# Separate slots for loads, half-size and whole staging in the last pass of a two-layer decode step with its gradients

## The chip, the core and the metric

The kernel runs on one core of one Trainium2 chip. The metric is device time in microseconds (us) of one launch; lower is better. The core has four compute engines with queues of their own (PE for matmuls, with its weight loads shown as PEld; DVE; ACT; POOL) and SP, which here only issues the loads. Sixteen DMA engines move data between the memory outside the core (HBM, called "dram" in the profile) and the on-chip memory of 128 partitions. PE writes its results to PSUM banks, from where DVE or ACT must fetch them.

## What is computed

The reference is two layers of a decode step (one token, batch 2), and the gradients of all its inputs. A layer is x + attention(layernorm(x)), then x + MLP(layernorm(x)); both layers use the same weights and the same caches.

```python
def _A_ref(x, k_cache, v_cache, wq, wo):      # x 2x1x1024; caches 2x4x16384x128
    q = (x @ wq) ...                          # 32 query heads on 4 cache heads
    scores = jnp.einsum("bhqd,bhkd->bhqk", q, k) * (Dh ** -0.5)
    p = _softmax(scores, axis=-1)
    o = jnp.einsum("bhqk,bhkd->bhqd", p, v)
    return ... o @ wo

def _B_ref(x, w1, b1, w2, b2):                # w1 1024x3584, w2 3584x1024
    y = _layernorm(x, axis=-1)
    h = _gelu(jnp.einsum("bsd,df->bsf", y, w1) + b1)
    return jnp.einsum("bsf,fd->bsd", h, w2) + b2

x = x + _A_ref(_layernorm(x), ...); x = x + _B_ref(_layernorm(x), ...)   # twice
_out, _vjp = jax.vjp(_f, A_x, A_k_cache, A_v_cache, A_wq, A_wo, B_w1, B_b1, B_w2, B_b2)
return (_out, *_vjp(grad_out))
```

All arrays are bf16. Both caches are 33.6 MB each, and so are their gradients (64 stores of 1 MB in all); the gradients of wq, wo, w1 and w2 are outer products of a few columns (2 layers x batch 2 = 4 columns), 31.5 MB together.

## The kernel before

**A program of pieces.** The kernel is first written down as a list of pieces (`P.emit(fn, uses)`): each piece is a Python function that issues a few instructions, with the chunks that it uses. A *chunk* is up to 1 MB of on-chip memory (128 partitions x 4,096 bf16 columns): a load of a part of a cache or a weight, a staging area for a result on its way out, or a small work area. `Program.keep` then looks where a chunk that is loaded again could stay on chip from its last use to the next: it counts the slots, takes off a reserve (`SPARE`, 5) and what lives at each piece, and keeps the shortest gaps first. `Program.run` walks the pieces, hands out slots and calls the functions. The order of the instructions in each engine's queue is therefore the order of the pieces (`tc.manual_schedule`); waits are put in from what touches what.

**Slots.** There are 15 slots of 1 MB (`slot_tiles`), and two areas of two slots each that are free only until a mark: half of `Et[1]` each until piece 683 and half of `D1t` each until piece 1295. In `run` all chunks stand in one list in the order of their first use, loads and staging alike. As soon as a slot is free, the next chunk of that list takes it, and if it is a load, its DMA is issued on SP's queue there and then. So a staging chunk takes its slot as many pieces ahead of use as a load does, and a load may take a slot that staging has just left; SP then waits until the store has landed, and with it every load behind.

**Passes.** Attention forward for layer 0 and 1 (`attn_fwd`), each followed by the MLP; then backward: the MLP of layer 1, attention of layer 1 (`attn_bwd(1, ...)`), the MLP of layer 0, and the last pass, attention of layer 0 (`attn_bwd(0, ..., outputs=outputs)`). An attention pass goes over the 8 pairs (batch, cache head) in 16 steps each; pass directions alternate (`up`, `down`), so the pair that ends a pass starts the next. In a backward step, `kblock` turns an eighth of a V chunk on DVE (L367) and multiplies it with PE (L380), and `direct` multiplies the K chunk's columns (L405) 16 steps later; `slope` and `exchange` (16 small ACT copies, L414) stand between. The backward blocks of wo and wq are turned with PE (L342) and copied by ACT or DVE (L217, L220).

**Outputs in the last pass.** `outputs(s, ...)` adds pieces to each step s:

- `kv_outputs`: for each pair, 8 chunks of cache gradient. `turn` builds a block (L1000), `unit` multiplies it with the work area `qc` (L1018), `cast_out` takes 512 columns from PSUM to the staging chunk on ACT (L225) or DVE (L228), whichever has less to do, and after 8 units POOL issues a 1 MB store (L1023).
- `dw_units`: weight gradients as outer products. `y_rows` transposes columns to 4 rows (L1034) and copies them to partitions 0 to 3 of a work chunk y (L1035) that `y_zero` has cleared (L1041, POOL); `x_rows` transposes the other factor to X (L1049), copied by ACT or DVE; a unit is one 512-column matmul over all 128 partitions (L1064) and a cast. `pieces_rows` groups 7 or 8 units to one store (L1087). `dbias` sums y's rows for the two biases (L1099, L1100, L1103).
- There are three y: `y1` for dh (gradient of w1), `y2` for the gradients of w2 and wo and for half of wq's, `y3` for the rest of wq's. The pieces of weight gradients wait in a list `bg` and are handed out by a credit of 1.3 or more a step, so that they end some 20 steps after the last cache gradient.

K(7,1) below means chunk 1 (of 4) of the K cache of pair 7; w2(24), wo(20) are the chunks of w2 and wo that start at block 24 and 20 of 128 rows. *Ahead* is a load that is issued and not yet used; a *lead* is the number of pieces between issue and first use.

Of the kernel before, what the change touches and what calls it, by code (L numbers as in the profile page):

```python
# [21 lines left out]
SPARE = 5  # L22
SKEW = 2
LAG_F = 28
LAG_B = 16
# [3 lines left out]
class Chunk:  # L29


    def __init__(self, load=None, key=None):
        self.load = load
        self.key = key
# [17 lines left out]
class Program:  # L52
# [6 lines left out]
    def chunk(self, load=None, key=None):  # L59
        c = Chunk(load, key)  # L60
        self.chunks.append(c)
        return c
# [39 lines left out]
    def run(self, slots):  # L102

        order = sorted((c for c in self.chunks if c.first is not None and c.into is None), key=lambda c: c.first)
        free = list(slots)
        nxt = 0
        for i, (fn, uses) in enumerate(self.ops):
            while nxt < len(order):
                c = order[nxt]
                fits = [s for s in free if s[1] is None or c.last < s[1]]  # L110
                s = min(fits, key=lambda s: 1 << 30 if s[1] is None else s[1], default=None)
                if s is None:
                    break
                free.remove(s)
                c.slot, c.at = s, s[0]
                if c.load is not None:
                    c.load(c.at)
                nxt += 1
            uses = [c.root() for c in uses]
            for c in uses:  # L120
                assert c.slot is not None, f"piece {i}: no slot for its chunk"
            fn()
            for c in uses:
                if c.last == i:
                    free.append(c.slot)
# [4 lines left out]
def kernel(  # L130
# [55 lines left out]
    xwp = ctx.enter_context(tc.tile_pool(name="xwp", bufs=2))  # L186
# [72 lines left out]
    D0t = pers.tile([128, 2 * 1024], BF16, name="ds0")  # L259
    slot_tiles = [pers.tile([128, CH], BF16, name=f"slot{i}") for i in range(NSLOT)]  # L260
# [10 lines left out]
    def columns(name, n):  # L271

        t = vec.tile([128, n * 4 + 124], BF16, name=name)
        V.memset(t[:, n * 4:], 0.0)
        wide[name[0]] = t
        return t[:, 0:n * 4].rearrange("p (j c) -> p j c", c=4)
# [683 lines left out]
    def kv_outputs(pos, g):  # L960
# [3 lines left out]
        qc = P.chunk()  # L964
# [25 lines left out]
        for n, (c, w) in enumerate([(c, w) for c in range(NCH) for w in range(2)]):  # L990
            stg = P.chunk()
# [37 lines left out]
    def y_rows(colT, j0, jn, y, at_):  # L1029

        def f():
            tp = ob().bitcast(BF16)[0:4, 0:jn * 128].rearrange("p (a b) -> p a b", b=128)
            for j in range(jn):
                PE.transpose(tp[:, j, :], colT[:, j0 + j, :], ident[:])  # L1034
            V.tensor_copy(out=y.ap[0:4, at_:at_ + jn * 128], in_=flat(tp))  # L1035
            dve(0.7)

        return f, [y]

    def y_zero(y, n):  # L1040
        return (lambda: GP.memset(y.ap[:, 0:n], 0.0)), [y]  # L1041

    def x_rows(xn, j0, jn, hold):
# [11 lines left out]
    def dw_units(xn, y, y_at, pieces):  # L1055
# [3 lines left out]
        for units, store in pieces:  # L1059
            stg = P.chunk()  # L1060
            for n, (j, c0, cn, at_) in enumerate(units):
                def f(j=j, c0=c0, cn=cn, at_=at_, last=(n == len(units) - 1), stg=stg, store=store):
                    ps = ob()[:, 0:cn]
                    PE.matmul(ps, lhsT=hold[j // 4 * 4][:, j % 4, :], rhs=y.ap[:, y_at + c0:y_at + c0 + cn], start=True,  # L1064
# [4 lines left out]
                todo.append((j, (f, [stg, y])))  # L1069
        res, built = [], set()  # L1070
        for n, (_, u) in enumerate(todo):
            for j, _ in todo[n:n + 4]:
                if j // 4 not in built:
                    built.add(j // 4)
                    res.append(x_rows(xn, j // 4 * 4, 4, hold))
# [3 lines left out]
    def pieces_rows(out_ap, n_in, n_out, c0=0):  # L1079

        rb = max(1, CH // n_out)
        res = []
        for j0 in range(0, n_in // 128, rb):
            units = [(j0 + j, c0 + c, 512, j * n_out + c) for j in range(rb) for c in range(0, n_out, 512)]

            def store(ap, j0=j0):
                GP.dma_start(out_ap[j0 * 128:(j0 + rb) * 128, c0:c0 + n_out].rearrange("(j p) n -> p j n", p=128),  # L1087
                             ap[:, 0:rb * n_out].rearrange("p (j n) -> p j n", j=rb))
# [4 lines left out]
    def dbias(y, y_at, n, out_ap):  # L1093
        c = P.chunk()
        res = []
        for c0 in range(0, n, 512):
            def f(c0=c0):
                ps = ob()[0:1, :]
                PE.matmul(ps, lhsT=ones_bf[:, 0:1], rhs=y.ap[:, y_at + c0:y_at + c0 + 512], start=True, stop=True)  # L1099
                V.tensor_copy(out=c.ap[0:1, c0:c0 + 512], in_=ps)  # L1100
                dve(0.6)
                if c0 + 512 >= n:
                    GP.dma_start(out_ap.rearrange("(o f) -> o f", o=1), c.ap[0:1, 0:n])  # L1103
            res.append((f, [c, y]))
# [119 lines left out]
    early += [y_zero(y1, F)] + [y_rows(dh_all, j0, min(8, FJ - j0), y1, j0 * 128) for j0 in range(0, FJ, 8)]  # L1224
    early += units[40:]
    early += dbias(y2, 0, D, out_9)
    early += dw_units("m", y1, 0, pieces_rows(out_6, D, F))
# [65 lines left out]
```

## Time and profile before

| | us |
|---|---|
| median of 3 runs (1266.1 to 1267.7) | 1266.45 |
| the profiled execution | 1268.7 |
| its span, first to last instruction | 1266.8 |

| busy over the span | us | share |
|---|---|---|
| PE | 931.8 | 74% |
| PEld | 709.6 | 56% |
| DVE | 782.8 | 62% |
| ACT | 590.2 | 47% |
| POOL | 73.2 | 6% |
| loads on SP's queue | 354.46 MB | 72.0% of 16 engines |
| stores on POOL's queue | 98.66 MB | 19.3% of 16 engines |

A row of engines by stage (busy us in a stretch, with the number of instructions in brackets) ends with the TensorE clock that was granted (1.00 is full speed), the mean busy share of the 16 DMA engines, and GB/s. A row of waits reads: the engine, its line, what it waited for; total us, times, longest. In a timeline a row reads: start, duration, engine, line, operation, output<-inputs, and in square brackets the idle time before it with what ended it.

### The profile page before, as it was taken

The page shows a single profiled execution, that of the slowest core. Times are in us where ns is not written, and L with a number is a line of the kernel's source. Part 1 is how long each engine was busy: PE and PEld are TensorE (multiplying, and loading weights), DVE is VectorE, ACT ScalarE, POOL GpSimd, SP SyncE. Part 2 cuts the span into 40 slices and gives each one's busy share as a digit, 9 for nine tenths or more (in the row PEclk, how much of TensorE's full clock was granted, in tenths as well). Part 3 has the DMA queues.
Part 4 walks back from the last instruction along what each step waited for, and adds up shares of the span by engine and source line. Part 5 has one row for each costly group of instructions (what it writes and reads, how often), then busy time and mean ns, then how long its engine had stood idle before and what let it go on. Part 6 is the DMA issues. An engine that isn't in the chain of part 4 may idle for free. (4 is left out here: it accounts for less than half of the span.)

```text
span 1266.8 us, 36604 instructions
## 1 busy us (share of the span) xinstructions
PE 931.8 (74%) x15799; PEld 709.6 (56%) x15809; DVE 782.8 (62%) x1630; ACT 590.2 (47%) x1484; POOL 73.2 (6%) x118
## 2 busy tenths in 40 slices
PE   4556655877865578788758977787787778888885
PEld 4555544777764477678757865454444444444342
DVE  5765662258876224767654466666676567877775
ACT  0411221203323112555543446766676666877764
POOL 0000000000000000000000100200110011111112
PEclk9855555755555557666757988888888788988898
DMA  9999999989999999799998855798999988999966
GB/s 357 413 414 414 413 414 412 378 326 354 411 414 413 413 397 396 278 415 411 415 413 330 326 171 201 279 388 351 365 335 336 374 339 322 375 388 377 346 275 232
DMA packets 97581, 455.44 MB, mean 360 GB/s; under 512 B 7138, under 2 KB 7138, under 8 KB 59148
## 3 DMA queue, kind: packets, MB, share of 16 engines
q1 hardware_dynamic: 80604, 354.46, 72.0%
q0 software_dynamic: 16816, 98.66, 19.3%
q8 instruction: 123, 2.02, 0.6%
q14 instruction: 38, 0.31, 0.1%
HBM read 354.47 MB, written 98.62 MB: 358 GB/s over the span
## 5 line engine op out<-in xcount | busy, mean ns | idle before, releaser
L367 DVE STREAM_TRANSPOSE kT<-slot 128x512 int32<-128x512 int32 x476 | 319.1, 695 | 104.0 <-PE sc L380 92.2
L380 PE MATMUL sc<-qbd,kT 128*128 128x32 bf16 x4096 | 273.7, 226 | 15.9 <-DVE kT L367 11.1
L380 PEld LDWEIGHTS <-kT 128*128 128x128 bf16 x4096 | 221.1, 118 | 59.4 <-issue 24.9
L405 PEld LDWEIGHTS <-slot 128*128 128x128 bf16 x3648 | 148.5, 104 | 132.1 <-issue 48.1
L405 PE MATMUL sb<-xt,slot 128*128 128x8 bf16 x3648 | 167.1, 177 | 64.3 <-DMA slot<-in_A_v_cache_dram 27.8
L225 ACT CAST slot<-sc 128x512 bf16<-128x512 f32 x310 | 177.5, 589 | 77.1 <-PE sc L1018 46.1
L228 DVE CAST slot<-sc 128x512 bf16<-128x512 f32 x213 | 144.5, 681 | 75.5 <-PE sc L1018 40.4
L217 ACT COPY kT<-tp 128x512 int32<-128x512 int32 (+1 forms) x165 | 95.9, 583 | 180.2 <-PE tp L342 168.2
L342 PE MATMUL tp<-ident,slot 128*128 128x128 bf16 x1800 | 171.0, 252 | 8.3 <-DVE kT L220 2.6
L1018 PE MATMUL sc<-slot,blk 128*128 128x512 bf16 x339 | 136.9, 428 | 33.4 <-ACT slot L225 20.4
L342 PEld LDWEIGHTS <-slot 128*128 128x128 bf16 x1800 | 133.6, 114 | 11.6 <-issue 5.6
L414 ACT COPY xt<-ds 32x64 int32<-32x64 int32 x512 | 123.9, 242 | 28.2 <-DVE ds L860 21.6
L581 ACT ACTIVATE e<-sc 128x512 bf16<-128x512 f32 x32 | 19.0, 597 | 228.7 <-DVE sc L578 180.1
L225 ACT CAST slot<-sb 128x512 bf16<-128x512 f32 x156 | 91.9, 589 | 35.8 <-PE sb L1018 14.5
L220 DVE COPY kT<-tp 128x1024 bf16<-128x1024 bf16 (+1 forms) x83 | 53.9, 650 | 82.6 <-PE tp L342 71.8
L1064 PE MATMUL sc<-slot,X 128*128 128x512 bf16 x159 | 66.2, 434 | 24.8 <-ACT slot L225 17.9
L228 DVE CAST slot<-sb 128x512 bf16<-128x512 f32 x105 | 71.6, 682 | 19.5 <-PE sb L1018 8.2
L414 ACT COPY xt<-e 32x128 int32<-32x128 int32 x256 | 75.6, 295 | 3.9
L1018 PE MATMUL sb<-slot,blk 128*128 128x512 bf16 x166 | 71.1, 428 | 5.7 <-DVE slot L228 2.0
L1018 PEld LDWEIGHTS <-blk 128*128 128x128 bf16 x512 | 45.7, 103 | 50.8 <-issue 39.8
L1023 POOL DMA_DIRECT2D out_dram<-slot x64 | 34.2, 535 | 360.5 <-ACT slot L225 226.4
L1064 PEld LDWEIGHTS <-X 128*128 128x128 bf16 x240 | 23.2, 103 | 32.9 <-issue 23.1
(271 smaller groups left out, 894.1 us busy)
## 6 DMA issues: line engine op xcount, KB each, us to landing
slot<-in_A_k_cache_dram SPq DMA_DIRECT2D x110, 1024.0 KB, 16.7
slot<-in_A_v_cache_dram SPq DMA_DIRECT2D x104, 1024.0 KB, 15.6
out_dram<-slot POOLq DMA_DIRECT2D x87, 1024.0 KB, 8.6
slot<-in_A_wq_dram SPq DMA_DIRECT2D x30, 1024.0 KB, 10.4
slot<-in_A_wo_dram SPq DMA_DIRECT2D x27, 1024.0 KB, 13.6
slot<-in_B_w_dram SPq DMA_DIRECT2D x19, 1024.0 KB, 12.1
slot<-in_B_w_dram SPq DMA_DIRECT2D x20, 896.0 KB, 16.0
ds<-in_A_v_cache_dram SPq DMA_DIRECT2D x8, 1024.0 KB, 18.1
```

The lines of the kernel that those rows point to most:

```text
L217: S.copy(out=dst.bitcast(I32), in_=src.bitcast(I32))
L220: V.tensor_copy(out=dst, in_=src)
L225: S.copy(out=dst, in_=src)
L228: V.tensor_copy(out=dst, in_=src)
L342: PE.transpose(tp[:, j, :], t, ident[:])
L367: V.transpose(out=kT[:].bitcast(I32).rearrange("p (w j m) -> p w j m", w=4, j=4), in_=c.ap[:, (i % 4) * 1024:(i % 4 + 1) * 1024].bitcast(I ...
L380: PE.matmul(sc[:, a0:a0 + 4, :, 2 * (i % 4) + q], lhsT=kv[:, 2 * q + w, :, e], rhs=qbd[:, g, 2 * w + e], start=(w == 0 and e == 0), stop=( ...
L405: PE.matmul(acc, lhsT=c.ap[:, n * 128:(n + 1) * 128], rhs=xv[:, i // 4, t // 2, :, 2 * (i % 4) + t % 2], start=(i == 0 and t == 0), stop=( ...
L414: S.copy(out=d[32 * t:32 * t + 32, c0:c0 + cn, j, :], in_=s[32 * j:32 * j + 32, c0:c0 + cn, t, :])
L1018: PE.matmul(ps, lhsT=hold["blk"][:, j, :], rhs=flat(qm(w)[:, (u % 2) * 4:(u % 2) * 4 + 4, :]), start=True, stop=True)
L1023: GP.dma_start((dKv if w == 0 else dVv)[g, :, c * 32:(c + 1) * 32, :], stg.ap.rearrange("p (t d) -> p t d", d=128))
L1064: PE.matmul(ps, lhsT=hold[j // 4 * 4][:, j % 4, :], rhs=y.ap[:, y_at + c0:y_at + c0 + cn], start=True, stop=True)
```

## The change

It touches the planner and the outputs of the last pass.

- Chunks have a kind: "load" (also y and the two rows of outputs), "half" (`qc`, staging of weight and bias gradients) or "full" (staging of cache gradients). A slot has a kind, a first piece and a last piece.
- Of the 15 slots, three are load slots until the first step of the last pass and then six half slots; four are load slots until step 19 of it (`LAG_O - 2`) and then full slots; eight stay load slots. The Et and D1t areas stay as they were.
- In `run` only loads (and y) take slots ahead, in order of first use. A staging chunk takes its slot at the piece that uses it first.
- `keep` counts load slots and load chunks only, and its reserve is 4 instead of 5.
- Weight gradients are stored from half slots: 62 stores of up to 0.5 MB instead of 31 of up to 1 MB. Bias gradients are stored 512 columns at a time: nine stores instead of two.
- y1, y2, y3 become one chunk `Y`, cleared once. Row group q of it (partitions 32q to 32q+3) holds the rows of w2's and wo's gradients (q = 0), dh (q = 1) and dq (q = 2), all columns side by side. So that a matmul over 128 partitions meets only its own group, X has zeros in all other partitions: X is now two lasting tiles `Xt`, cleared by POOL when their group changes, and the copy writes only 4 partitions. The column arrays have 64 zero columns in front so that a transpose can put the 4 columns at partition 32q.

```diff
-SPARE = 5
+SPARE = 4
+N_HALF = 3
+N_FULL = 4
...
     def keep(self, slots, spare):
-        room = [sum(1 for s in slots if s[1] is None or i < s[1]) - spare for i in range(n)]
+        room = [sum(1 for s in slots if s[1] == "load" and (s[3] is None or i < s[3])) - spare for i in range(n)]
...
-            if c.first is None:
+            if c.first is None or c.kind != "load":
                 continue
...
     def run(self, slots):
-        order = sorted((c for c in self.chunks if c.first is not None and c.into is None), key=lambda c: c.first)
-        free = list(slots)
+        order = sorted((c for c in self.chunks if c.first is not None and c.into is None and c.kind == "load"),
+                       key=lambda c: c.first)
+        free = {}
+        for s in slots:
+            free.setdefault(s[1], []).append(s)
         nxt = 0
+
+        def take(c, i):
+            fits = [s for s in free[c.kind] if i >= s[2] and (s[3] is None or c.last < s[3])]
+            s = min(fits, key=lambda s: 1 << 30 if s[3] is None else s[3], default=None)
+            if s is None:
+                return False
+            free[c.kind].remove(s)
+            c.slot, c.at = s, s[0]
+            if c.load is not None:
+                c.load(c.at)
+            return True
+
         for i, (fn, uses) in enumerate(self.ops):
...
+            while nxt < len(order) and take(order[nxt], i):
                 nxt += 1
             uses = [c.root() for c in uses]
             for c in uses:
-                assert c.slot is not None, f"piece {i}: no slot for its chunk"
+                if c.slot is None and c.kind != "load":
+                    take(c, i)
...
-        qc = P.chunk()
+        qc = P.chunk(kind="half")
...
-            stg = P.chunk()
+            stg = P.chunk(kind="full")
...
+    Y = P.chunk()
...
-            tp = ob().bitcast(BF16)[0:4, 0:jn * 128].rearrange("p (a b) -> p a b", b=128)
+            tp = ob().bitcast(BF16)[32 * q:32 * q + 4, 0:jn * 128].rearrange("p (a b) -> p a b", b=128)
...
-            V.tensor_copy(out=y.ap[0:4, at_:at_ + jn * 128], in_=flat(tp))
+            V.tensor_copy(out=Y.ap[32 * q:32 * q + 4, at_:at_ + jn * 128], in_=flat(tp))
...
+    def x_rows(xn, j0, jn, q, hold):
 
         def f():
-            X = xwp.tile([128, 4, 128], BF16, name="X")
+            xn_[0] += 1
+            b = xn_[0] % 2
+            if xq[b] != q:
+                GP.memset(Xt[b][:], 0.0)
+                xq[b] = q
...
-                PE.transpose(tp[:, j, :], wide[xn][:, 4 * (j0 + j):4 * (j0 + j) + 128], ident[:])
-            copy_bf(flat(X[:, 0:jn, :]), flat(tp), 0.36, 0.4)
-            hold[j0] = X
+                c0 = 64 + 4 * (j0 + j) - 32 * q
+                PE.transpose(tp[:, j, :], wide[xn][:, c0:c0 + 128], ident[:])
+            r = slice(32 * q, 32 * q + 4)
+            copy_bf(flat(Xt[b][r, 0:jn, :]), flat(tp[r]), 0.36, 0.4)
+            hold[j0] = Xt[b]
...
-            stg = P.chunk()
+            stg = P.chunk(kind="half")
...
-        rb = max(1, CH // n_out)
         res = []
-        for j0 in range(0, n_in // 128, rb):
-            units = [(j0 + j, c0 + c, 512, j * n_out + c) for j in range(rb) for c in range(0, n_out, 512)]
+        if n_out <= 1024:
+            parts = [(j0, 2, 0, n_out) for j0 in range(0, n_in // 128, 2)]
+        else:
+            parts = [(j0, 1, c, min(2048, n_out - c)) for j0 in range(n_in // 128) for c in range(0, n_out, 2048)]
+        for j0, rb, cb, cn in parts:
+            units = [(j0 + j, c0 + cb + c, 512, j * cn + c) for j in range(rb) for c in range(0, cn, 512)]
...
-    y1, y2, y3 = P.chunk(), P.chunk(), P.chunk()
-    early = [y_zero(y2, CH), y_rows(gM_all, 0, 8, y2, 0), y_rows(gA_all, 0, 8, y2, 1024)]
-    units = dw_units("h", y2, 0, pieces_rows(out_8, F, D))
+    early = [(lambda: GP.memset(Y.ap, 0.0), [Y]), y_rows(gM_all, 0, 8, 0, 0), y_rows(gA_all, 0, 8, 0, 1024)]
+    units = dw_units("h", 0, 0, pieces_rows(out_8, F, D))
...
+        if s == 0:
+            mark("half")()
+        if s == LAG_O - 2:
+            mark("full")()
...
-    slots = [(t[:], None) for t in slot_tiles]
-    slots += [(Et[1][:, i * CH:(i + 1) * CH], marks["e1"]) for i in range(2)]
-    slots += [(D1t[:, i * CH:(i + 1) * CH], marks["d1"]) for i in range(2)]
+    slots = []
+    for i, t in enumerate(slot_tiles):
+        until = marks["half"] if i < N_HALF else marks["full"] if i < N_HALF + N_FULL else None
+        slots.append((t[:], "load", 0, until))
+        if i < N_HALF:
+            slots += [(t[:, j * 2048:(j + 1) * 2048], "half", until, None) for j in range(2)]
+        elif i < N_HALF + N_FULL:
+            slots.append((t[:], "full", until, None))
+    slots += [(Et[1][:, i * CH:(i + 1) * CH], "load", 0, marks["e1"]) for i in range(2)]
+    slots += [(D1t[:, i * CH:(i + 1) * CH], "load", 0, marks["d1"]) for i in range(2)]
     P.keep(slots, SPARE)
```

More of the change, by code (lines that the diff above doesn't have):

```diff
@@ L29, with __init__ @@
 class Chunk:
-    def __init__(self, load=None, key=None):
+    def __init__(self, load=None, key=None, kind="load"):
         self.load = load
+        self.kind = kind
         self.key = key
@@ L57, in __init__, with chunk @@
         self.chunks = []
-    def chunk(self, load=None, key=None):
-        c = Chunk(load, key)
+    def chunk(self, load=None, key=None, kind="load"):
+        c = Chunk(load, key, kind)
         self.chunks.append(c)
@@ L120, in run @@
             for c in uses:
-                assert c.slot is not None, f"piece {i}: no slot for its chunk"
+                if c.slot is None and c.kind != "load":
+                    take(c, i)
+                assert c.slot is not None, f"piece {i}: no {c.kind} slot"
             fn()
@@ L124, in run @@
                 if c.last == i:
-                    free.append(c.slot)
+                    free[c.kind].append(c.slot)
                     c.slot = None
@@ L259 @@
     D0t = pers.tile([128, 2 * 1024], BF16, name="ds0")
+    Xt = [pers.tile([128, 4, 128], BF16, name=f"X{i}") for i in range(2)]
     slot_tiles = [pers.tile([128, CH], BF16, name=f"slot{i}") for i in range(NSLOT)]
@@ L1063, in f @@
                     ps = ob()[:, 0:cn]
-                    PE.matmul(ps, lhsT=hold[j // 4 * 4][:, j % 4, :], rhs=y.ap[:, y_at + c0:y_at + c0 + cn], start=True,
+                    PE.matmul(ps, lhsT=hold[j // 4 * 4][:, j % 4, :], rhs=Y.ap[:, y_at + c0:y_at + c0 + cn], start=True,
                               stop=True)
@@ L1068, in f @@
                         store(stg.ap)
-                todo.append((j, (f, [stg, y])))
+                todo.append((j, (f, [stg, Y])))
         res, built = [], set()
@@ L1074, in dw_units @@
                     built.add(j // 4)
-                    res.append(x_rows(xn, j // 4 * 4, 4, hold))
+                    res.append(x_rows(xn, j // 4 * 4, 4, q, hold))
             res.append(u)
@@ L1232 @@
         k = down[2 * i] % HKV
[L1233 to L1235 removed]
+        late[16 * (2 * i + 1) + LAG_B + 17] = [y_rows(dq_all, k * R, 8, 2, k * 1024)] + dw_units(
+            "n", 2, 0, pieces_rows(out_4, D, 1024, k * 1024))
     bg = list(early)
```

64 lines of the change are left out of this document (25 added, 39 removed).

## The prediction

> **What bounds the kernel now.** I read three views in this order: the page's slices and a table by stage, to see which stage has which limit; the waits of SP's queue and of PE in the last pass; then the clock around one stall. Stages by the lines that run in them: 0 to 500 us the two forward layers with their MLPs, 500 to 690 the backward attention of layer 1, 690 to 745 the backward MLP of layer 0, 745 to 1258 the last pass.
>
> ```profile
> core 0: us, PE busy (x) PEld busy (x) DVE busy (x) ACT busy (x) POOL busy (x), PEclk, DMA share, GB/s
> 275.00:440.00 165.00, 114.76 (x2505) 102.07 (x2504) 113.54 (x236) 47.35 (x144) 0.29 (x1) 0.50 1.00 401
> 500.00:690.00 190.00, 143.12 (x3066) 136.38 (x3065) 117.97 (x270) 95.28 (x314) 0.00 (x0) 0.65 0.97 385
> 690.00:745.00 55.00, 48.54 (x1023) 46.13 (x1020) 26.16 (x71) 20.79 (x36) 4.08 (x2) 0.94 0.71 261
> 745.00:1258.00 513.00, 408.81 (x4552) 228.89 (x4562) 362.49 (x659) 355.68 (x806) 61.29 (x98) 0.86 0.85 326
> ```
>
> The attention passes before 690 us keep the DMA engines full (share 0.97 to 1.00): they end when their bytes have come. 690 to 745 is PE's (48.5 of 55 us). In the last pass nothing is full: DMA 0.85, PE 409 of 513 us, DVE 362, ACT 356. It is made of a chain with stalls, so what counts is which stalls the change removes.
>
> ```profile
> engine line waited for: us in total, times, longest us
> SPq L306 <- DMA out_dram<-slot: 280.7, 29, 18.3
> SPq L311 <- DMA out_dram<-slot: 63.0, 5, 21.9
> ```
> ```profile
> PE sc L1018 <- ACT slot L225: 20.4, 12, 3.8
> PE sc L1064 <- ACT slot L225: 17.9, 8, 3.3
> PE sb L405 <- DMA slot<-in_A_k_cache_dram: 13.5, 5, 5.7
> ```
>
> These are the waits of SP's queue and of PE between 745 and 1258 us. SP issues the loads in order, and 34 times it stands still for 343.7 us in all, because the slot of the next load was last used for staging, whose store has not landed. But of these 344 us PE feels 13.5: the loads run about 55 pieces ahead. PE's two larger rows are ACT's casts queued behind the 16 copies of L414 (4 us each time); the change leaves those.
>
> ```profile
> 950.00:956.50 6.50, 6.27 (x88) 3.90 (x86) 5.81 (x10) 5.08 (x11) 0.53 (x1) 1.00 0.99 354
> 956.50:962.50 6.00, 0.33 (x3) 0.04 (x2) 1.36 (x3) 0.97 (x2) 0.53 (x1) 0.76 1.00 382
> 962.50:964.50 2.00, 2.00 (x26) 1.45 (x27) 0.85 (x2) 0.59 (x1) 0.00 (x0) 0.50 1.01 427
> 964.50:966.50 2.00, 2.00 (x15) 1.10 (x14) 1.26 (x2) 0.99 (x2) 0.53 (x1) 0.52 1.03 404
> 966.50:970.00 3.50, 3.24 (x44) 1.65 (x43) 3.17 (x7) 2.95 (x7) 0.00 (x0) 1.00 0.99 311
> ```
>
> Here PE waits 5.67 us for a K chunk. Afterwards the granted clock is 0.50 for 4 us with PE busy throughout: half of those 4 us, 2 us, is lost once more. The stalls that ended at 867.9 (3.26 us) and 991.4 (2.99 us) are followed by 4 us at 0.50 too.
>
> **1. Loads no longer wait for stores.** I worked through the planner's lists (keep, run) over the pieces in order. For before they give 345 loads, which is the page's count (341 large ones and 4 small), 38 of the last pass's 70 loads behind a store (the trace: 34 waits), and issue a median of 62 pieces ahead of use, 52 at least. The pass has 1,442 pieces in 512 us, 0.355 us each. So a lead of 55 pieces is 19.5 us; a wait of 343.7/34 = 10.1 us leaves 9.4, against 10.0 us from issue to landing (median of K's loads between 780 and 1220 us): just late, now and then, as the five stalls show. By the new rule no load follows a store, the median lead is 89 pieces (31.6 us), the least still 52 (18.5 us), now without the 10 us. Full gain: 13.5 us of stalls, plus 3 x 2 us of half clock, 19.5. The DMA engines limit it: 0.85 x 513 = 436 us of work in this pass, and between 820 and 1200 us their share is already 0.93, so some loads stay late. I take 14; bounds 0 and 19.5.
>
> **2. What is kept.** The reserve falls from 5 to 4 and staging is no longer counted. The lists give 27 kept chunks for 24, 342 loads for 345: gone are K(3,1) in the second forward layer, V(0,1) at the start of the backward one, and w2(24), wo(20), wo(24), V(3,0), which were loaded between 690 and 780 us; added are K(7,1) to K(7,3) early in the last pass. One load costs 1.05 MB/0.414 MB per ns = 2.53 us where DMA is full, so the first two give up to 5.1 us; the next four nothing (DMA share 0.71 and less there); the three added 7.6 us of DMA time, which the 0.85 hides (0.85 becomes 0.865), and which would be on the path if DMA were full. I take 3 gained; bounds 7.6 lost and 5.1 gained.
>
> **3. Kept chunks cost depth.** Chunks loaded ahead fall from 12 to 8 in the middle of the backward pass of layer 1 (pieces 1600 to 1700) and from 5-6 to 4 at its end; from 5 to 4 in the first MLP. I cost it at nothing: a lone 1 MB load lands in 4.8 us (740 to 785 us) and takes 2.53 us of full-rate time, so 3 in flight suffice. If not, it is the third rival.
>
> **4. One Y, lasting X.** Three memsets of Y (3.51 us for 4,096 columns, 3.10 for 3,584, 1.82 for 2,048) become one. The first hides in POOL's 31 us of idle time before 722 us; the third did not:
>
> ```profile
> 1241.05 1.82 POOL L1041 MEMSET slot<- 128x2048 bf16 x1
> 1242.91 0.68 DVE L1035 COPY slot<-sc 4x1024 bf16<-4x1024 bf16 x1 [3.17 <-POOL slot L1041]
> 1243.64 0.59 PE L1064 MATMUL sc<-slot,X 128*128 128x512 bf16 x1 [3.75 <-DVE slot L1035]
> ```
>
> POOL reaches it behind a store, DVE waits, PE stands for 3.75 us with nothing else left to do. I take 3 gained (bounds 0 and 4.8, with the half clock). Added are 8 memsets of X, two at each change of row group. From the three rows, (3.51-1.82)/2048 = 0.83 ns a column, so 0.55 us each, behind at most a store's 0.77 us. The copy into X, with the casts behind it on ACT or DVE and the matmuls that need those banks, waits for it. The pieces of X come up to four units before use; the first two memsets meet idle POOL. I take 2 lost; bounds 0 and 8 x 3.75 = 30. The four copies of dh now write rows of a Y that L1064 is reading, and hold the next L1064 for about 0.7 us each as at 748 us: 1 lost, bounds 0 and 3.
>
> **5. Half stores.** 31 gradient stores become 62 and two bias stores nine: 38 issues more on POOL, 0.77 us each (L1087), 29 us, hidden by POOL's idle time (61 of 513 us busy). Without that cover it would be 29 us. Nothing is queued behind them but other stores and the X memsets. The bytes are the same: DMA time 0 more, if it goes by bytes. Matmuls, casts and copies keep their number and width; the copy of X moves 4 partitions instead of 128 at the same width, so 0.
>
> **6. Staging taken late.** A cache chunk gets one of four whole slots at its first use; by the lists at least 47 pieces (16.7 us) after that slot's last store was issued, a gradient piece 46. Stores land in 8.9 us (median), 15.4 at most. So no wait: 0. If landings grew past 16.7 us the casts on ACT and DVE would wait instead of SP.
>
> **Sum:** -14 -3 -3 +2 +1 = -17 us. The profiled execution took 1268.7 us (span 1266.8 and 1.9 around it), 2.25 above the median of 1266.45, to which I apply the difference: 1249.
>
> **The rivals.**
> *A wait takes the place of the one removed* (chance 0.18). With SP unleashed the engines fill, stores land later than 16.7 us, ACT and DVE wait in L225 and L228; or loads stay late because DMA is full. For it: share 0.93 in the middle, store landings up to 15.4. Against it: 436 us of DMA work in 513. Then term 1 is nothing, and terms 2 and 4 remain: 1266.5 - 3 = 1263 (1260 to 1266).
> *More is gained than PE's row shows* (0.07): DMA idles at 0.42 to 0.64 between 740 and 780 us and around 810; earlier loads there also smooth later stretches. All bounds at their best: 19.5 + 5.1 + 4.8 = 29, or 1237.
> *Slower: too little depth at the turns* (0.17). In pieces 1773 to 1821 the leads fall from 62-91 to 24-48. At 0.343 us a piece (501 pieces in 172 us) 25 pieces are 8.6 us. The loads of wq between 545 and 640 us land in 16.6 us. If that stayed so with four in flight, the first is 8 us late, and four per 16.6 us is 4.15 us a chunk against 2.53: 12 chunks x 1.6 = 19. The turn of the first MLP (15 chunks) adds up to 24, of which PE's own pace hides about half. 8 + 19 + 12 = 39, less the 14 + 3 - 3 of the last pass, less nothing of term 2: 1291, or 1276 if only the later turn suffers. It decides from the point where four in flight no longer fill the engines. Against it: landings follow the number in flight, 19.9 us at about eight, 4.8 alone.
> *Half a store costs the engines a whole one's time* (0.04). Stores of 86.99 MB take 48.7% of 440 us (780 to 1220 us), 2.46 us per MB; the 31.5 MB of weight gradients 77 us. Twice that brings the pass's work to 436 + 77 = 513, all of its length: with the idle starts some 1290. For it: 4 KB stores still take 3.9 us to land. Against it: that is time to landing, not engine time, and 896 KB and 1,024 KB land in the same 8.6 us. The Trainium skill ("DMA: Bandwidth & Descriptors", Bandwidth, Measured) advises batches of 1 MiB or more for three quarters of the peak, and its Anatomy of one DMA gives a fixed 2.0 us per transfer: by that, an estimated 31 x 2 = 62 us if nothing overlapped them. The stores here overlap with loads at a share of 0.93, and no run here shows half ones yet.
>
> **How the numbers follow.** Forecast 0.54: 1249, own range 1240 to 1258. The range to the other cases: 1234 (all bounds at best, a little beyond) to 1278 (the slower rival with one turn); beyond it lie most of two-turn starvation, the half stores and a rest, under 2 in 10. 0.2% is 2.5 us, about what this kernel's measurement can tell from none. Faster than 1263.9: 0.54 + 0.07 + 0.10 of the first rival = 0.71; same: the first rival's other 0.07; slower: 0.17 + 0.04 + 0.01 = 0.22.
>
> **What would show it.** Right: no SPq row for stores in the last pass; PE's L405 row for K under 4 us; DMA share of the last pass near 0.88; 3 loads fewer; no stall near the second gradient group of wq. Wrong: L225 or L228 waiting for out_dram stores; new PE rows for DMA between 640 and 700 us or around 220 to 280; ACT or DVE waiting for POOL in the copies of X; the time above 1264.

## The result, and the profile after

The changed kernel takes 1250.38 us (median of 4 runs, 1249.42 to 1252.42) against 1266.28 for the kernel before beside it: a ratio of 0.9875, with a 95% interval of 0.9858 to 0.9892. The profiled execution took 1252.42, its span is 1250.3. In the changed kernel the lines named above have moved by 10 to 25: V's turn is L379, V's matmul L392, K's L417, the casts L235 and L238, the copies L227 and L230, the cache-gradient unit L1030 and its store L1035, y's copy L1049, X's memset L1063, the weight-gradient unit L1084 and its store L1110, the bias copy L1125.

Stages first, as before: stretch, its length, busy us of PE, PEld, DVE, ACT, POOL (instructions), granted clock, share of the DMA engines, GB/s.

```profile
core 0: us, PE busy (x) PEld busy (x) DVE busy (x) ACT busy (x) POOL busy (x), PEclk, DMA share, GB/s
275.00:440.00 165.00, 113.75 (x2502) 101.10 (x2499) 112.96 (x236) 47.35 (x144) 0.69 (x1) 0.51 1.02 410
...
500.00:690.00 190.00, 144.88 (x3051) 138.52 (x3049) 115.85 (x261) 95.35 (x314) 0.00 (x0) 0.62 0.96 381
690.00:745.00 55.00, 48.16 (x991) 45.98 (x989) 26.89 (x72) 19.76 (x35) 4.54 (x3) 0.94 0.66 239
```

The stages ahead of the last pass look the same, with a slightly lower clock (0.62 for 0.65) between 500 and 690 us. The last pass is cut more finely, by what runs: from its first to its last V matmul (L380, then L392), to the last cache-gradient unit (L1018, then L1030), to the end of the span. Of the kernel before:

```profile
747.10:1167.50 420.40, 332.83 (x3938) 193.18 (x3944) 295.57 (x538) 296.08 (x687) 45.96 (x76) 0.86 0.87 335
1167.50:1230.80 63.30, 54.31 (x505) 26.74 (x504) 47.70 (x90) 43.99 (x89) 8.41 (x14) 0.89 0.85 321
1230.80:1266.80 36.00, 21.92 (x105) 8.37 (x104) 20.35 (x31) 16.55 (x31) 8.21 (x10) 0.86 0.61 234
```

And of the changed kernel:

```profile
750.70:1153.30 402.60, 329.90 (x3938) 191.37 (x3943) 296.51 (x533) 295.45 (x690) 62.38 (x108) 0.86 0.93 362
1153.30:1219.70 66.40, 55.59 (x507) 26.84 (x505) 47.48 (x90) 44.27 (x91) 12.46 (x21) 0.90 0.65 262
1219.70:1250.30 30.60, 19.94 (x104) 7.74 (x104) 19.93 (x30) 17.05 (x32) 10.35 (x15) 0.96 0.71 274
```

The 16.5 us between the spans are a sum of four signed parts (each from one execution; the four runs of the changed kernel lie 3.0 us apart, so a part of two or three us by itself is not clear of noise): the last pass starts 3.6 us later (750.7 for 747.1); its main stretch is 17.8 shorter, 14.9 of it idle time of PE (420.4 - 332.8 = 87.6 us became 72.7); the stretch of the last units is 3.1 longer; the rest is 5.4 shorter. In that last part the last weight-gradient unit comes 22.9 us after the last cache-gradient unit instead of 27.6.

SP's queue over the whole span (line, what it waited for: us, times, longest), its two largest rows:

```profile
SPq L318 <- DVE kT L379: 317.8, 56, 21.7
SPq L1321 <- DMA out_dram<-slot: 96.8, 2, 93.5
```

The 343.7 us behind stores are gone from the last pass. SP now waits for the users of its slots, which is what it means to run ahead, and for stores only at the end of the program (L1321). PE has no row for a K chunk in the last pass; before it was 13.5 us. In their place stand small new rows (700 to 1250 us):

```profile
ACT X L227 <- POOL X L1063: 6.6, 6, 1.9
PE sc L1030 <- ACT X L227: 5.7, 4, 2.5
...
PE sc L1030 <- DVE slot L1125: 4.2, 4, 2.1
DVE slot L1125 <- DMA out_dram<-slot: 3.6, 2, 2.4
DVE slot L238 <- DMA out_dram<-slot: 1.9, 1, 1.9
ACT slot L235 <- DMA out_dram<-slot: 0.9, 1, 0.9
```

ACT waits for POOL's memsets of X and PE for ACT; a bias copy on DVE waits for a half slot's store and PE for DVE. The two casts of the cache gradients wait for a store once each, 2.8 us together.

### The profile page after: what moved, and what is told of

Its sections match the earlier page's. It is cut to its first block, busy times and chain, and to the rows that moved or that the text cites. A ratio compares the mean times of both kernels' runs of the same rounds, so it can differ in the third digit from the quotient of the medians.

```text
span 1250.3 us, 36696 instructions
## 1 busy us (share of the span) xinstructions
PE 933.0 (75%) x15801; PEld 712.6 (57%) x15809; DVE 783.5 (63%) x1630; ACT 590.2 (47%) x1488; POOL 96.2 (8%) x162
## 3 DMA queue, kind: packets, MB, share of 16 engines
HBM read 351.32 MB, written 98.62 MB: 360 GB/s over the span
## 5 line engine op out<-in xcount | busy, mean ns | idle before, releaser
L379 DVE STREAM_TRANSPOSE kT<-slot 128x512 int32<-128x512 int32 x476 | 318.7, 694 | 111.4 <-PE sc L392 101.9
L392 PE MATMUL sc<-qbd,kT 128*128 128x32 bf16 x4096 | 276.4, 227 | 15.2 <-DVE kT L379 10.4
L392 PEld LDWEIGHTS <-kT 128*128 128x128 bf16 x4096 | 223.7, 119 | 56.2 <-issue 23.2
L417 PEld LDWEIGHTS <-slot 128*128 128x128 bf16 x3648 | 149.9, 104 | 123.8 <-issue 56.4
L235 ACT CAST slot<-sc 128x512 bf16<-128x512 f32 x313 | 178.6, 588 | 62.6 <-PE sc L1030 30.7
L417 PE MATMUL sb<-xt,slot 128*128 128x8 bf16 x3648 | 167.3, 177 | 53.0 <-DMA slot<-in_A_v_cache_dram 27.1
L227 ACT COPY kT<-tp 128x512 int32<-128x512 int32 (+1 forms) x160 | 92.8, 582 | 176.2 <-PE tp L354 169.8
L238 DVE CAST slot<-sc 128x512 bf16<-128x512 f32 x205 | 138.0, 680 | 39.6 <-PE sc L1030 13.1
L1030 PE MATMUL sc<-slot,blk 128*128 128x512 bf16 x335 | 135.5, 429 | 28.3 <-ACT slot L235 8.3
L230 DVE COPY kT<-tp 128x1024 bf16<-128x1024 bf16 (+1 forms) x88 | 57.4, 652 | 82.9 <-PE tp L354 71.7
L235 ACT CAST slot<-sb 128x512 bf16<-128x512 f32 x152 | 89.4, 588 | 29.9 <-PE sb L1030 14.1
L238 DVE CAST slot<-sb 128x512 bf16<-128x512 f32 x114 | 77.8, 683 | 35.6 <-PE sb L1030 16.8
L1030 PE MATMUL sb<-slot,blk 128*128 128x512 bf16 x173 | 72.2, 417 | 9.2 <-DVE slot L238 4.5
L1030 PEld LDWEIGHTS <-blk 128*128 128x128 bf16 x512 | 45.4, 103 | 57.0 <-issue 47.7
L1084 PE MATMUL sc<-slot,X 128*128 128x512 bf16 x152 | 61.2, 416 | 13.4 <-ACT slot L235 8.6
L1035 POOL DMA_DIRECT2D out_dram<-slot x64 | 34.7, 542 | 276.4 <-ACT slot L235 197.6
L1110 POOL DMA_DIRECT2D out_dram<-slot x62 | 41.9, 675 | 143.7 <-ACT slot L235 125.7
## 6 DMA issues: line engine op xcount, KB each, us to landing
slot<-in_A_wq_dram SPq DMA_DIRECT2D x31, 1024.0 KB, 11.4
slot<-in_B_w_dram SPq DMA_DIRECT2D x21, 896.0 KB, 13.2
```

The source lines that it names most:

```text
L227: S.copy(out=dst.bitcast(I32), in_=src.bitcast(I32))
L230: V.tensor_copy(out=dst, in_=src)
L235: S.copy(out=dst, in_=src)
L238: V.tensor_copy(out=dst, in_=src)
L379: V.transpose(out=kT[:].bitcast(I32).rearrange("p (w j m) -> p w j m", w=4, j=4), in_=c.ap[:, (i % 4) * 1024:(i % 4 + 1) * 1024].bitcast(I ...
L392: PE.matmul(sc[:, a0:a0 + 4, :, 2 * (i % 4) + q], lhsT=kv[:, 2 * q + w, :, e], rhs=qbd[:, g, 2 * w + e], start=(w == 0 and e == 0), stop=( ...
```

## The experiments

Every ratio is to the kernel before on the same chip. Unless said otherwise an edit is against the changed kernel. "Main stretch" and "last units" are the first two stretches above.

### One Y without slots of its own: e1_old_slots, e5_slots_held

The first takes the slots' kinds away again (reserve 5, whole stores) and keeps one Y and the lasting X. The second also holds two idle chunks from y1's and y3's first piece to their last, so that one Y gives no slot back.

```diff
-SPARE = 4
+SPARE = 5
-        self.kind = kind
+        self.kind = "load"
...
-            parts = [(j0, 2, 0, n_out) for j0 in range(0, n_in // 128, 2)]
+            parts = [(j0, 4, 0, n_out) for j0 in range(0, n_in // 128, 4)]
...
+        slots.append((t[:], "load", 0, None))
```
```diff
+    h1, h3 = P.chunk(), P.chunk()
+    def held(units, h):
+        return [(fn, list(us) + [h]) for fn, us in units]
...
-    early += dw_units("m", 1, 0, pieces_rows(out_6, D, F))
+    early += held(dw_units("m", 1, 0, pieces_rows(out_6, D, F)), h1)
```

> One Y, the lasting X and its memsets as in the changed kernel, but the slots, the reserve and the whole stores of before (345 loads, staging in the common list). My theory: the gain comes from SP no longer waiting for stores. Then this kernel is back at the time of before: about 320 us of SP's waits for stores return, PE waits some 13 us for K again; from 1266.3 the tail's memset stall comes off (4.7 us) and the waits for X's memsets come on (some 6 us): 1267, between 1262 and 1271. Rival: the gain comes from the outputs (one Y, no memset at the end, X copied in 4 partitions). Then it stays near 1250.

> e1_old_slots with two slots held idle for as long as the y1 and y3 of before held theirs; nothing is written there. e1 was 1258, faster than my theory had it. By the planner's lists the loads' median lead in the last pass is 62 pieces before, 75 in e1 and 61.5 here. Theory: the y chunks cost slots, and e1's gain beside the tail is the two slots that one Y gives back: 1263 to 1267 here, with the rows of the last pass's sixths as before. Rival: the gain is in the memsets and copies that are gone: it stays at 1256 to 1260.

e1 took 1258.17, ratio 0.9914 (0.989 to 0.9937), faster than expected; e5 1264.38, ratio 0.997 (0.9949 to 0.999), as expected. SP's and PE's rows of e1 in the last pass:

```profile
SPq L318 <- DMA out_dram<-slot: 311.4, 37, 15.9
...
SPq L323 <- DMA out_dram<-slot: 36.1, 3, 12.8
```
```profile
PE sb L417 <- DMA slot<-in_A_k_cache_dram: 13.0, 4, 5.7
```

SP's store waits and PE's K row are as large as before, yet e1's main stretch is 414.5 us for 420.4. In e5 it is 419.8 (e1 first):

```profile
747.60:1162.10 414.50, 328.47 (x3940) 190.11 (x3944) 296.58 (x534) 295.75 (x690) 44.88 (x79) 0.86 0.90 340
```
```profile
747.70:1167.50 419.80, 329.13 (x3939) 189.59 (x3944) 296.07 (x534) 296.19 (x690) 44.91 (x79) 0.86 0.88 336
```

So what one Y gains in that stretch, 5.3 us, are the two slots that it gives back: by the planner's lists the median lead is 62 pieces before, 75 in e1 and 61.5 in e5, and the intervals of the two ratios don't meet. In both kernels the last weight-gradient unit comes 22.9 us after the last cache-gradient unit, as in the changed kernel: that gain of 4.7 us comes with one Y and not with the slots, and is put down to the missing memset of y3 (PE's stall of 3.75 us). And from e1 to the changed kernel the main stretch falls by another 11.9 (414.5 to 402.6): that is what the slots of their own are worth. Neither the reserve nor the size of the stores makes this difference: e2 below, with the reserve of e1, takes 401.2 us there, and e8, with whole stores, 400.5.

### The reserve and the turn into the last pass: e2_reserve5, e7_reserve7

The changed kernel keeps more chunks and loads fewer ahead. With a larger reserve it keeps fewer: `SPARE = 5`, then `SPARE = 7` (17 kept, 352 loads).

> The changed kernel with a reserve of 5 instead of 4: 24 kept chunks, 345 loads; it loads K(3,1), V(0,1) and wo(20) again and is one chunk deeper ahead. Theory A (depth): the last pass started 3.6 us later in the changed kernel because only four chunks are ahead at the end of the backward pass of layer 1; with one more the last pass starts at 748 to 750 us instead of 750.7, and the time is 1248 to 1250. Rival (kept loads are what counts): the last pass starts 2 to 5 us later, and the time is 1252 to 1256.

> The changed kernel with a reserve of 7: 17 kept chunks, 352 loads, and 8 to 11 chunks ahead near the end of the backward pass of layer 1 where the changed kernel has 4 to 8 (before: 8 to 12). Theory (depth): the stretch from the first wo block to the last wq block of that pass, 190.4 us in the changed kernel and 187.8 before, falls to 187 to 189, and the last pass starts by 750 in spite of more loads; 1248 to 1254 in all. Rival (bytes): ten loads more cost up to 10 x 2.53 us where the DMA engines are full: 1258 to 1275, with the stretch as long as in the changed kernel or longer.

e2 took 1252.15, ratio 0.9869 (0.9846 to 0.9892), and its last pass starts at 754.5, later rather than earlier; by itself it spoke for the rival. e7 took 1248.15, ratio 0.9846 (0.9819 to 0.9872). PE's K row between 600 and 692 us, in the changed kernel, in e2 and in e7:

```profile
PE sb L417 <- DMA slot<-in_A_k_cache_dram: 15.5, 6, 3.6
```
```profile
PE sb L417 <- DMA slot<-in_A_k_cache_dram: 18.7, 9, 4.0
```
```profile
PE sb L417 <- DMA slot<-in_A_k_cache_dram: 12.8, 5, 3.5
```

Before, the row was 13.2 us. The backward attention of layer 1, from its first wo block to its last wq block, takes 187.8 us before, 190.4 in the changed kernel, 191.5 in e2, 187.8 in e7, whose last pass starts at 747.1, as before. Over all the kernels of this study that stretch takes 187.6 to 188.3 us in those with reserve 7 or more, or the old slots with reserve 5, and 190.0 to 192.6 in all with the new slots and reserve 4 or 5. So depth is what is missing there, and a reserve of 5 with seven slots set apart isn't yet enough. The two ratios alone would not settle it (their intervals overlap); the start of the pass does: 749.2 to 752.6 us in the five kernels with reserve 4, 746.7 to 748.5 in the four with reserve 7.

e7 reads 361.81 MB for 351.32, ten loads more, and is no slower. This doesn't say what a load costs where the engines are full, because the ten went elsewhere. Between 215 and 275, 440 and 500, 500 and 550, and 690 and 745 us the DMA share of the changed kernel is 0.85, 0.95, 0.84 and 0.66, and there e7 moves 41, 41, 53 and 41 GB/s more: about 9.8 of the 10.5 MB.

### X cleared early, biases stored together: e3_clear_early, e4_bias_stage, e6_clear_and_bias

The stall of PE at 1192 us in the changed kernel (start, duration, engine, line, operation; idle time before it and what ended it):

```profile
1190.35 0.55 POOL L1035 DMA_DIRECT2D out_dram<-slot  x1 [1.55 <-PE sc L1068]
1190.89 0.54 POOL L1063 MEMSET X<- 128x512 bf16 x1
1191.47 0.36 ACT L227 COPY X<-sc 4x256 int32<-4x256 int32 x1 [1.93 <-POOL X L1063]
...
1192.11 0.59 PE L1030 MATMUL sc<-slot,blk 128*128 128x512 bf16 x2 [2.52 <-ACT X L227]
```

POOL comes to the memset behind a store that had to wait first, ACT stands still for the memset with its casts behind the copy, and PE has no free bank. The clock around it:

```profile
1190.00:1192.00 2.00, 0.00 (x0) 0.11 (x2) 0.00 (x0) 0.36 (x1) 1.08 (x2) 1.00 0.66 262
...
1193.00:1196.00 3.00, 2.88 (x21) 1.26 (x21) 1.46 (x4) 1.60 (x4) 0.00 (x0) 0.53 0.33 137
1196.00:1199.00 3.00, 2.78 (x17) 0.98 (x16) 2.65 (x5) 2.26 (x5) 0.37 (x1) 0.90 0.00 0
```

The 2.52 us stall is paid again: from about 1 us after it PE runs at 0.53, in a stretch where it is busy 2.88 of 3 us. In e3 six of the eight memsets become pieces of their own right behind the last use of that X, where POOL has time; e4 puts four bias sums into a half slot and stores them together; e6 does both.

```diff
+    def x_clear(b, q):
+        def f():
+            GP.memset(Xt[b][:], 0.0)
+            xq[b] = q
+        return f, ()
...
+                if nxt is not None and j // 4 >= todo[-1][0] // 4 - 1:
+                    res.append(x_clear(xb[0] % 2, nxt))
```
```diff
-            c = P.chunk(kind="half")
+            if c0 % 2048 == 0:
+                c = P.chunk(kind="half")
...
-                GP.dma_start(out_ap.rearrange("(o f) -> o f", o=1)[:, c0:c0 + 512], c.ap[0:1, 0:512])
+                if c0 + 512 >= min(n, b0 + 2048):
+                    GP.dma_start(out_ap.rearrange("(o f) -> o f", o=1)[:, b0:c0 + 512], c.ap[0:1, 0:c0 + 512 - b0])
```

> The changed kernel with the six later memsets of X put right behind the last use of that X, one block of units ahead of the copy that needs it. Theory: the rows ACT X <- POOL X (6.6 us) and PE L1030 <- ACT X (5.7 us, some of it followed by half clock) vanish, and 4 to 7 us with them: 1243 to 1247. Rival: these waits only stand in for PSUM and cast waits that come anyway: 1249 to 1251.

> The changed kernel with the bias gradients staged four sums to a half slot (three stores instead of nine). Theory: in the changed kernel the seven sums for b1 take a half slot each one after the other, so a slot comes round again before its store has landed; the rows DVE L1125 <- DMA out_dram (3.6 us) and PE L1030 <- DVE L1125 (4.2 us) vanish: 1245 to 1248. Rival: the same time is spent waiting elsewhere: 1249 to 1251.

> e3 and e4 together on the changed kernel. If the two waits are separate: 1239.7 less 2 to 3, so 1236 to 1238. If e3 has already taken what e4 gives (its trace shows no wait of L1125 for stores): 1239 to 1241.

e3 took 1239.73, ratio 0.9768 (0.9746 to 0.9791), more gain than expected. Its only row of this kind left:

```profile
ACT X L227 <- POOL X L1072: 0.6, 1, 0.6
```

Its main stretch and last units, to be read against those of the changed kernel:

```profile
749.20:1144.80 395.60, 326.48 (x3939) 191.29 (x3943) 296.46 (x539) 295.53 (x685) 62.34 (x108) 0.88 0.94 368
1144.80:1206.80 62.00, 53.43 (x508) 26.19 (x505) 46.57 (x89) 43.77 (x90) 12.30 (x20) 0.92 0.70 283
```

They are 7.0 and 4.4 us shorter. PE's idle time falls by 3.6 and 2.2 (72.7 to 69.1 and 10.8 to 8.6), near the 5.7 us of the row; PE's busy time for the same work falls by 3.4 and 2.2, with the clock up from 0.86 to 0.88 and from 0.90 to 0.92. By these two executions half of the gain would be the clock that no longer falls. But the clock also differs between executions that have the same stalls. e7 has the row of 5.7 us too, and its two stretches are:

```profile
747.10:1148.90 401.80, 327.84 (x3941) 190.44 (x3946) 296.04 (x533) 295.89 (x691) 62.38 (x108) 0.88 0.92 360
1148.90:1214.20 65.30, 53.92 (x505) 26.31 (x502) 47.05 (x89) 44.29 (x90) 12.40 (x21) 0.92 0.67 270
```

Against e7 the busy time falls by only 1.4 and 0.5, the idle time by 4.9 and 2.8. The shorter idle time is shown; the clock adds something between 2 and 6 us.

e4 took 1247.72, as expected, ratio 0.9836 (0.9811 to 0.986), its main stretch 3.2 shorter, without a row for stores; its interval still touches that of the changed kernel. e6 took 1236.25, ratio 0.9761 (0.9731 to 0.9791), not to be told from e3, and the interval takes in both expectations. The traces speak for the second: with X cleared early the bias copies already meet landed stores (e3 shows no wait of its bias copies), and the main stretch is 394.7 us for 395.6, so e4's gain is not there twice.

### Whole stores: e8_whole_stores

Weight gradients in whole slots again, 31 stores; six whole staging slots beside one for `qc`, the same seven slots in all.

```diff
-N_HALF = 3
-N_FULL = 4
+N_HALF = 1
+N_FULL = 6
...
-            stg = P.chunk(kind="half")
+            stg = P.chunk(kind="full")
```

> The changed kernel with whole stores for weight and bias gradients (31 of up to 1 MB and 2), staged in full slots (two half slots are left for the work area, six full ones): the half stores undone, the slots still apart. Theory: a half store costs the DMA engines half a whole one's time, so nothing changes beside the bias staging, which is as in before: 1246 to 1250. Rival (half stores cost more): it is 5 us or more faster than e4, 1243 or less, at a lower DMA share in the last pass.

It took 1251.14, ratio 0.9861 (0.9835 to 0.9887), a little above what either theory had: no gain, so the half stores cost nothing that this can measure. The rows of stores (times, KB each, median us to landing), in the changed kernel and in e8:

```profile
out_dram<-slot POOLq DMA_DIRECT2D x64, 1024.0 KB, 9.3
...
out_dram<-slot POOLq DMA_DIRECT2D x54, 512.0 KB, 6.6
```
```profile
out_dram<-slot POOLq DMA_DIRECT2D x87, 1024.0 KB, 8.8
```

A half store lands in 6.6 us, more than half of 9.3, but landing is not engine time. The shares show it: in the main stretch, 0.93 in both kernels, the store queue's packets took 46.5% of 402.6 us for 74.94 MB in the changed kernel and 46.6% of 400.5 us for 74.88 MB in e8, 2.5 us per MB in both. The estimate of 62 us that the prediction worked out from the Trainium skill ("DMA: Bandwidth & Descriptors", Anatomy of one DMA) was for stores that nothing overlaps. Here they overlap, and it doesn't come.

### Both mended, with more reserve: e9_reserve7, e10_reserve10

e6 with `SPARE = 7`, then `SPARE = 10` (9 kept, 360 loads).

> e6 (early clearing and shared bias staging) with a reserve of 7. e7 showed that ten loads more cost nothing and that the depth at the end of the backward pass of layer 1 gives 2 to 4 us: 1232 to 1236, the last pass starting near 747. Rival: with the last pass shorter the added loads of its start get in the way: 1236 to 1240.

> The same with a reserve of 10: 9 kept chunks, 360 loads. Depth theory: beyond what the turn needs, depth gives no more, and 8 loads at 2.53 us are added to passes whose DMA engines are full: 1236 to 1250. If even these are free: as e9 within 2 us.

e9 took 1236.04, ratio 0.9742 (0.9722 to 0.9761), at the border of its two expectations. It has the lowest ratio of the study and beats the kernel before and the changed one, whose interval begins at 0.9858; from e6, e3 and e11 below it can't be told, their intervals overlap with its own. Its last pass starts at 746.7 (e6: 751.1) and its main stretch takes 394.7, as in e6. So the larger reserve shows in the start of the pass, and its gain in time, here as in e7, is too small for the ratios. e10 took 1240.07, ratio 0.9776 (0.9756 to 0.9797), whose interval overlaps e9's a little. There the MLP of forward layer 1 starts at 446.9 instead of 444.9, and the last pass at 751.5 instead of 746.7: the eight further loads fall partly where the DMA engines are full (share 1.03 for 0.93 between 215 and 275 us).

### When staging would wait: e11_three_full, e12_two_full

e9 with `N_FULL = 3`, then 2: a cache-gradient slot comes round after fewer pieces, while loads get the slots.

> e9 with three whole staging slots instead of four and nine slots for loads. By the lists a slot comes round 32 pieces after its last store was issued at the least, 47 in the median (11 and 16 us), against landings of 9.3 us in the median and 14.7 at most in the changed kernel. A few casts wait: rows of ACT and DVE for out_dram of 5 to 20 us, time 0 to 5 us above e9.

> The same with two whole staging slots: 17 pieces at the least, 26 in the median (6 and 9 us), so about half of the 64 cache stores have not landed when the slot is wanted. This is the first rival of the prediction made to happen: the wait for stores moves from SP to ACT and DVE, 30 x 2 to 4 us or 60 to 120 us of waits, of which PE feels a part: 15 to 60 us above e9.

e11 took 1237.49, ratio 0.9756 (0.9734 to 0.9779), not to be told from e9, with 4.0 us of waits where 5 to 20 were expected; e12 1284.65, ratio 1.0129 (1.0103 to 1.0154). The casts of e11 and of e12, waiting for stores:

```profile
ACT slot L235 <- DMA out_dram<-slot: 2.3, 1, 2.3
DVE slot L238 <- DMA out_dram<-slot: 1.7, 1, 1.7
```
```profile
DVE slot L238 <- DMA out_dram<-slot: 43.9, 18, 5.7
ACT slot L235 <- DMA out_dram<-slot: 37.5, 17, 5.3
```

With two slots the wait that the prediction's first rival described is real: 35 waits, 81.4 us, and the time is 48.6 us above e9's, both as expected. By the planner's lists a slot then comes round after 17 pieces at least and 26 in the median, at 0.355 us a piece 6 and 9.2 us, about what a store takes to land (a median of 6.1 us in e12, 9.3 in the changed kernel).

## Why the prediction was right, and where it was not

The forecast of 1249 was 1.4 us off, and its largest term was right: where the time went is where it said. That the total came so near is in good part luck. The profiled spans of the kernel before, e5, e1 and the changed kernel are 1266.8, 1263.2, 1259.1 and 1250.3 us. The first two steps are the new outputs and the slots that one Y returns: 7.7 us gained, where term 4 adds up to nothing (-3 +2 +1). The last step is all the rest, terms 1, 2, 3, 5 and 6: 8.8 us gained, where the forecast has 17. The two errors cancel. By the ratios, each known to some 0.2%, the luck is larger still: 0.9914 in e1 leaves only about 5 us for the last step.

Term by term, in the profiled spans:

| step of the prediction | forecast | measured | shown by |
|---|---|---|---|
| 1 loads free of stores | -14 | -11.9; -14.0 with whole stores | main stretch, e1 to the changed kernel and to e8 |
| 2 fewer loads, 3 depth for nothing | -3 | +3.6 | start of the last pass; e7 takes it back |
| 4 no memset of y3 | -3 | -4.7 | last weight-gradient unit, e1 and e5 |
| 4 slots that one Y returns | not in the sum | -5.3 | main stretch, e5 to e1 |
| 4 memsets of X | +2 | +11.4 | what e3 takes off the changed kernel: 7.0 and 4.4 |
| 4 copies of dh | +1 | PE waits 1.5 us for all copies of Y | the rows |
| 5 half stores | 0 | 0 | e8 |
| 5 nine bias stores | 0 | +3.2 | e4, main stretch |
| 6 staging taken late | 0 | 2.8 us of waits | the rows; e11, e12 |

The rows don't add up to one sum: each is a difference to another kernel, and +11.4 and +3.2 were taken off the changed kernel. In e5, which has the memsets of X and the old slots, the main stretch is 0.6 us shorter than before and the last units 1.5 longer. Yet PE's row for the copy of X is the same 5.7 us in e5, in e1 and in the changed kernel, so the stall was paid there too, and the new outputs must gain some us elsewhere. In the main stretch of e5 PE's waits for casts are 51.3 us for 55.3 before, and its busy time is 3.7 us less; why is open, and early clearing was not run with the old slots. One path adds up: the main stretch goes 420.4, 419.8 (e5), 414.5 (e1), 402.6, and 395.6 (e3).

**Step 1** held with its size. PE's idle time in the main stretch falls by 13.3 from e1 to the changed kernel (86.0 to 72.7), against the 13.5 of the row. The 6 us of half clock that its full gain also counted don't show: PE's busy time there is 328.5 in e1 and 329.9 in the changed kernel. The forecast sign, a DMA share near 0.88 in the last pass, came out at 0.87, but unevenly: 0.93 while the loads run, 0.65 in the last units, when they are through.

**Steps 2 and 3** failed, in the place that the third rival named and not at its size. "3 in flight suffice" was worked out from a chunk that landed alone in 4.8 us; at the end of the backward attention they do not suffice, but the loss is 2.6 us in that stretch and 1.0 around it (0.3 ahead, 0.7 behind), not the 25 to 40 of the rival, and the forward turns show none (the MLP of forward layer 1 starts at 444.1 us, before at 444.5). The saved loads were priced at 2.53 us each by the engines' rate, up to 5.1 us for two; the forward one was to come off ahead of 445 us, where 0.4 us did, less than the five kernels with reserve 4 differ there (442.1 to 445.5). No run here shows a load's price by itself: e7's ten cost nothing where the engines had room, and with e10's eight, some of them where they were full, the time rose by 4 us, at the edge of what the ratios can tell.

**Step 4** was right in the tail, and left out what a freed megabyte does while loads are late. For the memsets it took 0.55 us each and found 0.54, but "two lost" was the copy's own wait. The price is the chain: a memset behind a store that waits, a copy behind the memset, the casts behind the copy, PE's banks behind the casts, and then the clock. How much the clock adds is not settled. The prediction had that bound, 30 us, and chose too near to nothing.

**Step 5** counted the bias stores' issues on POOL but not their slots: nine sums that were kept in two chunks now take nine half slots, of which there are six, `qc` in one of them.

**Step 6** and the first rival: four slots hold, three nearly, two do not. The wait moves from SP to ACT and DVE only when a slot comes round about as fast as a store lands.

Two of the signs named for being wrong came as well, and a third in part: casts waiting for stores (2.8 us), ACT waiting for POOL in the copies of X (6.6), and a longer K row before 692 us (15.5 for 13.2). The second was the one that mattered.

## What to carry to other kernels

When loads and stores share slots, a store that hasn't landed holds up the whole load queue; give staging slots of its own, as few as let a slot come round later than its store lands (here four hold and two cost 48.6 us against four). A clear or a copy that an in-order engine reaches only when it is needed should be issued behind the last use of its target. And a chunk that is kept on chip is paid for in loads that can't run ahead. Look first at where its load would fall: ten loads in stretches where the engines had room cost nothing here.

## What was not expected of the hardware

The clock fell after a short stall: 2.52 us of idle PE at 1192 us were followed by 0.53 in the stretch 1193 to 1196. The Trainium skill ("TensorE: Matmul & The Clock Gate", What's actually happening) speaks of an idle window of about 3.4 us; this trace doesn't agree if that means idle throughout, the shorter gap was enough.

Whether the mean granted clock of a run is near 0.73 or near 0.80 says little here. The four runs of the changed kernel had 0.794, 0.802, 0.728 and 0.799, and took 1252.42, 1249.96, 1250.8 and 1249.42 us. (Within the upper group it says more: in ten runs of the kernel before beside e1 to e4 the time goes from 1272.84 us at 0.786 to 1260.07 at 0.808, not without exceptions; what causes what is open.) The traces show where the large difference sits: in the first 215 us the granted clock is 0.62 in the kernel before and 1.00 in the changed one, with PE busy 124.4 and 125.2 us on 2,674 matmuls each. The DMA share there is 1.00 and 1.01, and the MLP that follows starts at 221.1 and 221.2 us.
